# Opening loads of a fused attention and gated-MLP kernel: the first x tile in column halves from both queues, a new order of the first weight blocks, and a TensorE order to match

## The chip, the cores and the metric

The kernel runs on one core of one Trainium2 chip. The metric is the device time of one execution in microseconds. Before the change it is 206.2 us. The change touches only the first 6 us of the program and one later load, so everything here is about tenths of a microsecond; that is less than what one execution differs from the next, and part of the work is to tell the two apart.

## The reference, cut to what matters

```python
def _A_ref(x, wqkv, w_phi, wo):          # S=2048, D=512, H=32 heads of 16
    q, k, v = split(x @ wqkv)
    pq = einsum('bhsd,hdf->bhsf', q, w_phi)      # the kernel folds w_phi into wq and wk
    ...
def _B_ref(x, w_in, w_sp, b_sp, w_out):  # F = 1376 = 2*688
    z = gelu(x @ w_in)
    z1 = z[..., :688]
    z2 = layernorm(z[..., 688:])
    g = einsum('ts,bsf->btf', w_sp, z2) + b_sp
    return (z1 * g) @ w_out
g = sigmoid((x * gate_w).sum(-1, keepdims=True))
out = g * A + (1 - g) * B
```

The kernel starts with z2, the second half of `x @ w_in`. For that it needs x tiles transposed (`xT`) and four blocks of 128 rows of `w_in`, called blocks 0 to 3 of `w_z2` (172 KB each). The gate's weights ride along as one more column of `w_z2`: a small matmul turns `gate_w` into a column, and a copy puts it there.

## The kernel before

The opening loads, as issued from two queues (SyncE's, `nc.sync`, and ScalarE's, `nc.scalar`):

```python
nc.sync.dma_start(out=xs[:, 0, :], in_=x2[0:P, :])          # x tile 0, 128 KB
nc.scalar.dma_start(out=xs[:, 1, :], in_=x2[P:2 * P, :])    # x tile 1
load_z2w(nc.sync, 0)                                        # block 0 of w_z2
load_z2w(nc.scalar, 1)
load_z2w(nc.sync, 2)
nc.scalar.dma_start(out=gaterow[0:NDT, :], in_=gate_w...)
load_z2w(nc.sync, 3)
# ... a dummy gelu, to load ScalarE's table
x_dma_T(2, 2)            # transposing load of x tiles 2 and 3, SyncE
for h in range(2): ...   # w_z1, two loads, SyncE
for i in range(4, 8): x_dma_T(i)
# ... more transposing loads; brow; wqkT (two); w_phi (eight small loads); wv (two); w_sp
```

The opening on TensorE. `x_T` transposes pieces of an x tile into PSUM and a copy on VectorE (once ScalarE) brings them to `xT`; `one(t, b, j)` is the matmul of tile t, block b, column half j; `z_part` is half 1 of block 0 without the gate column, so that it needs no gate.

```python
warm_up(6)               # matmuls of constants, 512 columns
warm_up(1, P)            # and one of 128
x_T(0, 0, 1, ...); x_T(0, 1, NDT, ...)      # x tile 0
x_T(1, 0, 2, ...); x_T(1, 2, NDT, ..., on_act=True)
one(0, 0, 0); z_part(0, 0, HF, True)
gate_T()                 # gate column; the 345-column matmuls need its copy
one(0, 1, 0)
one(1, 0, 0); z_part(1, 0, HF, True)
one(1, 1, 0)
for tt in range(2): one(tt, 1, 1)           # the first with 345 columns
# ... blocks 2 and 3, then tiles 2, 3, ...
```

Much later, at 26 us, `fold` multiplies `wqkT` by `w_phi`; its first four matmuls together read all eight of the small w_phi loads.

The softmax here doesn't subtract the row's maximum and nothing guards it: scores larger than these inputs give would overflow.

## Time and profile before

| | before |
|---|---|
| time, median of 3 runs | 206.21 us (205.93 to 206.35) |
| TensorE busy | 200.8 of 204.5 us |
| first useful matmul | 4.54 us |
| tile 2's first matmul | 7.12 us |
| last w_phi landing; first fold matmul | 25.56; 25.93 us |

Two lines of the page: TensorE's busy time and the chain that ended last. TensorE (PE) is the chain, so every tenth that it starts later is paid at the end.

```profile
PE 200.8 (98%) x1557; PEld 119.9 (59%) x1557; DVE 130.4 (64%) x283; ACT 74.8 (37%) x122; POOL 45.6 (22%) x76
...
PE 98%; DVE 0%; issue 0%
```

Times inside an execution are counted from its first instruction. In text and tables the zero lies up to 0.01 us earlier than in the lines shown, so the last digit can differ by one.

The timeline of TensorE in the opening. Columns: start, duration of the group (us), engine, source line, operation, operands, count, and in brackets the idle time before it.

```profile
0.84 2.83 PE L222 MATMUL zp<-const-bfloat16-1.0 128*128 128x512 bf16 x7 [0.84 <-PEq L628]
3.46 0.63 PE L280 MATMUL pq<-ident,xs 128*128 128x128 bf16 x4
...
4.53 0.44 PE L191 MATMUL zp<-w_z,xT 128*128 128x344 bf16 x1
4.77 0.38 PE L230 MATMUL zp<-w_z,xT 128*128 128x344 bf16 x1
4.99 0.17 PE L290 MATMUL pq<-ident,gaterow 128*128 128x4 bf16 x1
5.02 0.45 PE L191 MATMUL zp<-w_z,xT 128*128 128x344 bf16 x2
```

A matmul's duration in the trace is longer than the step to the next one (0.31 us for a transpose here, where the next starts after 0.107), so waits are read from the distance between starts. The last transpose starts at 4.21 and the first useful matmul at 4.54: it waited for block 0, which the trace's semaphore events show landing at 4.50.

DMA traffic in the same stretch (columns: window, busy time of five engines, granted clock, DMA share, GB/s).

```profile
1.80:2.40 0.60, 0.60 (x3) 0.15 (x2) 0.48 (x3) 0.06 (x1) 0.56 (x4) 1.00 0.57 191
2.40:3.00 0.60, 0.60 (x3) 0.22 (x2) 0.00 (x0) 0.60 (x1) 0.24 (x1) 1.00 1.09 330
3.00:3.60 0.60, 0.60 (x5) 0.23 (x4) 0.00 (x0) 0.60 (x1) 0.00 (x0) 1.00 0.93 306
```

SyncE's queue, from the timeline: how long it takes to issue its loads. A plain load of 128 rows takes about 0.4 us to issue, a transposing load 1.2 us or more (the last of x 2.8); each is issued as soon as the one before is out, until the w_phi loads at 20 to 24 us.

```profile
0.81 0.39 SPq L119 DMA_DIRECT2D xs<-in_A_x_dram  x1
1.25 1.36 SPq L117 DMA_DIRECT2D w_z<-in_B_w_in_dram  x3
2.66 1.33 SPq L131 DMA_TRANSPOSE xT<-in_A_x_dram  x1
...
20.25 4.13 SPq L150 DMA_DIRECT2D wphi<-in_A_w_phi_dram  x8
```

### The profile page before, as it was taken

The page shows a single profiled execution, that of the slowest core. Times are in us where ns is not written, and L with a number is a line of the kernel's source. Part 1 is how long each engine was busy: PE and PEld are TensorE (multiplying, and loading weights), DVE is VectorE, ACT ScalarE, POOL GpSimd, SP SyncE. Part 2 cuts the span into 40 slices and gives each one's busy share as a digit, 9 for nine tenths or more (in the row PEclk, how much of TensorE's full clock was granted, in tenths as well). Part 3 has the DMA queues.
Part 4 walks back from the last instruction along what each step waited for, and adds up shares of the span by engine and source line. Part 5 has one row for each costly group of instructions (what it writes and reads, how often), then busy time and mean ns, then how long its engine had stood idle before and what let it go on. Part 6 is the DMA issues. An engine that isn't in the chain of part 4 may idle for free.

```text
span 204.5 us, 3996 instructions
## 1 busy us (share of the span) xinstructions
PE 200.8 (98%) x1557; PEld 119.9 (59%) x1557; DVE 130.4 (64%) x283; ACT 74.8 (37%) x122; POOL 45.6 (22%) x76
## 2 busy tenths in 40 slices
PE   8999999999999999999999999999999999999994
PEld 4666666655665555656565666555555555665642
DVE  4567484837977587979797789555566645633332
ACT  3566678796222333332424042222251136002303
POOL 3020202021523325334242442222204220200000
PEclk9999999999999999999999999999999999999999
DMA  6999699999999027940423219853567458552833
GB/s 194 252 205 171 80 151 290 146 278 247 256 249 213 3 38 182 287 94 16 75 48 45 51 38 120 154 109 64 105 161 80 90 113 183 63 96 51 156 64 104
DMA packets 89931, 27.22 MB, mean 133 GB/s; under 512 B 84184, under 2 KB 89912, under 8 KB 89912
## 3 DMA queue, kind: packets, MB, share of 16 engines
q1 hardware_dynamic: 87744, 24.99, 65.4%
q10 hardware_dynamic: 2168, 1.98, 3.5%
q8 instruction: 12, 0.20, 0.4%
q14 instruction: 7, 0.06, 0.1%
HBM read 4.15 MB, written 2.10 MB: 31 GB/s over the span
## 4 chain that ended last, share of the span: by engine, by line
PE 98%; DVE 0%; issue 0%
PE mm L454 37%; PE zp L191 18%; PE mm L355 14%; PE mm L515 9%; PE mm L509 7%; PE mm L395 7%; PE kvacc L411 2%; PE at L467 2%; PE zp L222 1%; PE mm L520 1%; PE zp L307 0%; PE pq L280 0%; PE at L478 0%; PE pq L307 0%; DVE ob L527 0%; PE zp L230 0%
## 5 line engine op out<-in xcount | busy, mean ns | idle before, releaser
L454 PE MATMUL mm<-z2all,wspT 128*128 128x344 bf16 x512 | 79.9, 309 | 0.0
L454 PEld LDWEIGHTS <-wspT 128*128 128x128 bf16 x512 | 49.0, 98 | 25.3
L191 PE MATMUL zp<-w_z,xT 128*128 128x344 bf16 (+1 forms) x254 | 38.1, 310 | 0.0
L359 ACT ACTIVATE eq<-mm 128x512 bf16<-128x512 f32 x32 | 17.4, 594 | 51.4 <-PE mm L355 25.7
L363 DVE TENSOR_REDUCE zs<-eq 128x64 f32<-128x1024 bf16 x16 | 19.5, 1220 | 20.0 <-ACT eq L359 20.0
L191 PEld LDWEIGHTS <-xT 128*128 128x128 bf16 x254 | 24.4, 98 | 11.8
L359 ACT ACTIVATE ek<-mm 128x512 bf16<-128x512 f32 x32 | 17.3, 600 | 27.1 <-PE mm L355 27.1
L459 DVE SCALAR_TENSOR_TENSOR ucat<-mm,bT,z1all 128x344 bf16<-128x344 f32 x32 | 17.4, 544 | 15.0 <-PE mm L454 15.0
L372 POOL TENSOR_TENSOR eq<-eq,ratio 128x512 bf16<-128x512 bf16 x16 | 16.9, 1055 | 44.6 <-DVE ratio L371 36.7
L531 ACT ACTIVATE ob<-mm,g_inv 128x512 bf16<-128x512 f32 (+1 forms) x15 | 10.1, 680 | 33.1 <-PE mm L520 28.5
L363 DVE TENSOR_REDUCE zs<-ek 128x64 f32<-128x1024 bf16 x16 | 19.3, 1209 | 2.8 <-ACT ek L359 2.8
L515 PE MATMUL mm<-wspT,uT 128*128 128x512 bf16 (+2 forms) x85 | 20.1, 367 | 0.0
L355 PEld LDWEIGHTS <-xT 128*128 128x128 bf16 x128 | 12.2, 98 | 12.0
L372 POOL TENSOR_TENSOR ek<-ek,ratio 128x512 bf16<-128x512 bf16 x16 | 16.9, 1056 | 2.2 <-DVE ratio L371 1.7
L509 PE MATMUL mm<-wspT,oT 128*128 128x512 bf16 (+2 forms) x68 | 16.6, 366 | 0.0
L355 PE MATMUL mm<-wq_p,xT 128*128 128x512 bf16 x64 | 16.4, 379 | 0.0
L395 PE MATMUL mm<-wv_sb,xT 128*128 128x512 bf16 x64 | 16.4, 379 | 0.0
L355 PE MATMUL mm<-wk_p,xT 128*128 128x512 bf16 x64 | 16.3, 379 | 0.0
L209 DVE BATCH_NORM_STATS2 bn<-z2all 128x6 f32<-128x344 bf16 x32 | 14.9, 501 | 0.0
L206 ACT ACTIVATE z2all<-zp 128x688 bf16<-128x688 f32 x16 | 11.8, 744 | 7.3 <-PE zp L191 7.2
L260 ACT ACTIVATE z1all<-zp 128x688 bf16<-128x688 f32 x16 | 11.9, 744 | 5.1 <-PE zp L191 4.6
L515 PEld LDWEIGHTS <-uT 128*128 128x128 bf16 x85 | 8.1, 98 | 9.4 <-issue 0.2
(77 smaller groups left out, 142.7 us busy)
## 6 DMA issues: line engine op xcount, KB each, us to landing
out_dram<-ob ACTq DMA_DIRECT2D x12, 128.0 KB, 2.4
wspT<-in_B_w_out_dram SPq DMA_DIRECT2D x2, 640.0 KB, 4.9
w_z<-in_B_w_in_dram SPq DMA_DIRECT2D x2, 344.0 KB, 4.7
w_z<-in_B_w_in_dram SPq DMA_DIRECT2D x3, 172.0 KB, 3.5
wv_sb<-in_A_wqkv_dram SPq DMA_DIRECT2D x2, 256.0 KB, 2.7
wspT<-in_A_wo_dram SPq DMA_DIRECT2D x2, 256.0 KB, 4.0
out_dram<-ob SPq DMA_DIRECT2D x3, 128.0 KB, 1.8
uT<-ucat SPq DMA_TRANSPOSE x16, 2.8
```

The source lines that it names most:

```text
L191: nc.tensor.matmul(zp[:, j, 0:n], lhsT=xT[:, dt, tt * P:(tt + 1) * P], rhs=wt[:, dt, j * HF:j * HF + n], start=(dt == 0), stop=(dt == NDT ...
L209: nc.vector.bn_stats(out=bn6[:, tt, j, :], in_=z2v[:, j, :])
L260: nc.scalar.activation(out=z1all[:, tt, :].rearrange("p (j n) -> p j n", j=2), in_=zp[:, :, 0:HF], func=AF.Gelu_apprx_tanh,)
L355: nc.tensor.matmul(ps[:, :], lhsT=xT[:, dt, tt * P:(tt + 1) * P], rhs=w[:, dt, :], start=(dt == 0), stop=(dt == NDT - 1))
L359: nc.scalar.activation(out=e[:, :, a, :], in_=ps[:, :].rearrange("p (h f) -> p h f", f=DH), func=AF.Exp, scale=1.0 - 2.0 * a)
L363: nc.vector.tensor_reduce(out=z[:].rearrange("p h a -> p (h a)"), in_=e[:].rearrange("p h a f -> p (h a) f"), axis=AX.X, op=ALU.add,)
L372: nc.gpsimd.tensor_tensor(out=e[:, :, 1, :], in0=e[:, :, 1, :], in1=ratio[:, :, None].to_broadcast([P, H, DH]), op=ALU.mult)
L395: nc.tensor.matmul(v_ps[:, :], lhsT=xT[:, dt, tt * P:(tt + 1) * P], rhs=wv_sb[:, dt, :], start=(dt == 0), stop=(dt == NDT - 1))
L454: nc.tensor.matmul(gp[:, 0:HF], lhsT=wspT[:, st, tt * P:(tt + 1) * P], rhs=z2all[:, st, j * HF:(j + 1) * HF], start=(st == 0), stop=(st == ...
L459: nc.vector.scalar_tensor_tensor(out=ucat[tt % NU][:, c0 + j * HF:c0 + (j + 1) * HF], in0=gp[:, 0:HF], scalar=bT[:, tt:tt + 1], in1=z1all[ ...
L509: nc.tensor.matmul(acc, lhsT=oTs[tt][:, g, :], rhs=wo_t[:, g, c0:c1], start=start and g == 0, stop=stop and g == NG - 1)
L515: nc.tensor.matmul(acc, lhsT=uTs[tt][:, i + ft, :], rhs=w_main[i][:, ft, c0:c1], start=start and ft == 0, stop=False)
```

## The change

Its intent: 128 KB instead of 256 KB of x ahead of the first transposes; tile 1 and block 0 travel beside each other, and TensorE does both tiles' block 0 before the gate. The two loads of wv become one.

```diff
-    nc.sync.dma_start(out=xs[:, 0, :], in_=x2[0:P, :])
-    nc.scalar.dma_start(out=xs[:, 1, :], in_=x2[P:2 * P, :])
-    load_z2w(nc.sync, 0)
-    load_z2w(nc.scalar, 1)
+    HD = D // 2
+    nc.sync.dma_start(out=xs[:, 0, 0:HD], in_=x2[0:P, 0:HD])
+    nc.scalar.dma_start(out=xs[:, 0, HD:D], in_=x2[0:P, HD:D])
+    nc.sync.dma_start(out=xs[:, 1, :], in_=x2[P:2 * P, :])
+    load_z2w(nc.scalar, 0)
+    load_z2w(nc.sync, 1)
+    nc.scalar.dma_start(out=gaterow[0:NDT, :], in_=gate_w...)
     load_z2w(nc.sync, 2)
-    nc.scalar.dma_start(out=gaterow[0:NDT, :], in_=gate_w...)
-    load_z2w(nc.sync, 3)
+    load_z2w(nc.scalar, 3)
 ...
-    for h in range(2):
-        nc.sync.dma_start(out=wv_sb[:, 2 * h:2 * h + 2, :], in_=A_wqkv[...])
+    nc.sync.dma_start(out=wv_sb[:, :, :], in_=A_wqkv[...])
 ...
-        warm_up(6)
-        warm_up(1, P)
-        x_T(0, 0, 1, ...); x_T(0, 1, NDT, ...)
+        warm_up(5)
+        warm_up(3, P)
+        x_T(0, 0, 2, ...); x_T(0, 2, NDT, ...)
+        warm_up(2, P)
         x_T(1, 0, 2, ...); x_T(1, 2, NDT, ..., on_act=True)
         one(0, 0, 0); z_part(0, 0, HF, True)
+        one(1, 0, 0); z_part(1, 0, HF, True)
         gate_T()
         one(0, 1, 0)
-        one(1, 0, 0); z_part(1, 0, HF, True)
         one(1, 1, 0)
```

More of the change, by code (lines that the diff above doesn't have):

```diff
@@ L117, in load_z2w @@
         eng.dma_start(out=w_z2[:, dt, 0:FH], in_=w_in_v[:, dt, FH:F])
-    nc.sync.dma_start(out=xs[:, 0, :], in_=x2[0:P, :])
-    nc.scalar.dma_start(out=xs[:, 1, :], in_=x2[P:2 * P, :])
-    load_z2w(nc.sync, 0)
-    load_z2w(nc.scalar, 1)
+    HD = D // 2
[4 more added lines that the diff above has]
+    load_z2w(nc.sync, 1)
+    nc.scalar.dma_start(out=gaterow[0:NDT, :], in_=gate_w.rearrange("(dt p) -> dt p", p=P))
     load_z2w(nc.sync, 2)
-    nc.scalar.dma_start(out=gaterow[0:NDT, :], in_=gate_w.rearrange("(dt p) -> dt p", p=P))
-    load_z2w(nc.sync, 3)
+    load_z2w(nc.scalar, 3)
     scrap = early.tile([P, 1], BF16, name="scrap")
@@ L150 @@
         nc.sync.dma_start(out=wphi[us, :, us], in_=heads[u])
-    for h in range(2):
-        nc.sync.dma_start(
-            out=wv_sb[:, 2 * h:2 * h + 2, :],
-            in_=A_wqkv[h * 2 * P:(h + 1) * 2 * P, 2 * D:3 * D].rearrange("(dt p) n -> p dt n", p=P),
-        )
+    nc.sync.dma_start(out=wv_sb[:, :, :], in_=A_wqkv[:, 2 * D:3 * D].rearrange("(dt p) n -> p dt n", p=P))
     for q in range(NCH):
@@ L232, in z_part @@
                 rhs=w_z2[:, 0, HF + c0:HF + c1], start=start, stop=False, skip_group_check=True)
-        warm_up(6)
-        warm_up(1, P)
-        x_T(0, 0, 1, pq_tile([P, 1, P], BF16)[:, :, :])
-        x_T(0, 1, NDT, pq_tile([P, 3, P], BF16)[:, :, :])
+        warm_up(5)
+        warm_up(3, P)
+        x_T(0, 0, 2, pq_tile([P, 2, P], BF16)[:, :, :])
+        x_T(0, 2, NDT, pq_tile([P, 2, P], BF16)[:, :, :])
+        warm_up(2, P)
         x_T(1, 0, 2, tp1[:, :, :])
@@ L241, in z2_first_two @@
         z_part(0, 0, HF, True)
+        one(1, 0, 0)
+        z_part(1, 0, HF, True)
         gate_T()
         one(0, 1, 0)
-        one(1, 0, 0)
-        z_part(1, 0, HF, True)
         one(1, 1, 0)
```

## The prediction

> **What bounds it now.** TensorE: busy 200.8 of 204.5 us, 98% of the chain that ended last (page of the profile). A change at the opening counts only by how much it moves the TensorE stream, 1:1 to the end.
>
> **The opening now (timeline, waits).** Warm-up matmuls run from 0.84 to 3.36 us. The x tiles' DMAs land at 3.41 (SyncE) and 3.58 (ScalarE); eight transposes issue 3.46 to 4.32; block 0 of w_z2 lands at 4.50 and the first useful matmul starts at 4.54. It waits for block 0. Clock: warm-ups of 512 columns come every 427 ns, transposes of 128 every 107 ns, both half rate; from about 4.73 a 344-column matmul comes every 145 ns. The Trainium skill, "TensorE: Matmul & The Clock Gate", Part 1, says the array starts at half rate and doubles after about 3.4 us of activity; the trace agrees (about 3.9 us). So time won before 4.73 is worth half. A second loss: the gate matmul waits for gaterow, about 0.08 us (weight load at 4.92).
>
> **What the change does there.** 128 KB of x instead of 256 KB stand before tile 0's landing; DMA moves about 310 GB/s from 1.84 us (windows), landing about 0.7 us after its bytes. Estimates: x tile 0 lands at 3.0 to 3.3, tile 1 at 3.8, block 0 at 4.1, block 1 at 4.9, block 2 at 5.6, block 3 at 5.3. Transposes start at about 3.25, the first useful matmul at about 4.3, 0.2 us earlier, half of it in slow clock; with the gate wait gone TensorE is 0.15 to 0.2 us ahead from 5 us on. The Trainium skill, "DMA: Bandwidth & Descriptors", Issuing engines are not separate DMA queues, says both queues share the same 16 engines; so I expect no bandwidth gain, only another order.
>
> **What it costs.** There are eight completion semaphores in rotation. Before, seven DMAs precede the transposing load of x tiles 2 and 3, which issues at 2.66 without waiting. Now eight precede it, and in the instruction order it waits for ScalarE's x half to land (3.1 to 3.3). SyncE's queue issues back to back until 24.4 us (its issue of one transposing load takes 1.2 us), so everything behind shifts by about 0.4 to 0.6 us. Most has slack: tiles 2 and 3 land at 6.77 by bandwidth, w_z1 needed later. But the last of eight w_phi loads lands at 25.56, and the first fold matmul starts at 25.93; TensorE's sequencer waited for that landing until 25.59. Slack is about 0.26 us, less with TensorE 0.2 us early. DMA is partly idle near 11.5 us (0.2 to 0.5 busy), so the shift isn't absorbed by a backlog. The fold then starts at 25.9 to 26.3: opening gain lost, up to 0.3 us of stall net. Merging the two wv loads comes behind w_phi: no effect (wv lands 27.2, needed after 44 us), but it keeps later semaphores in the same rotation.
>
> **Prediction.** 206.35 us, 80% range 205.85 to 206.75. Faster by over 2%: 0.005; within 2%: 0.985; slower by over 2%: 0.01.
>
> **What would show it.** Right: first useful matmul at 4.2 to 4.4; gate matmul without idle time; tiles 2 and 3's load issued at 3.1 to 3.3; last w_phi landing at 25.9 to 26.1; a TensorE gap of 0.2 to 0.5 us before the first fold; after it the stream 0 to 0.3 us later than before. Wrong: w_phi lands at 25.6 as before, no gap at the fold; then about 206.0.
>
> **What would make it wrong.** SyncE's delay absorbed where transposing loads are already blocked (the loads at 11.87 and 15.37 took 2.4 to 2.8 us to issue); ScalarE's half landing before 2.9; tile 1 or block 2 landing late, stalling TensorE and delaying the clock; run-to-run spread of 0.4 us hiding everything.

## The result

| | before | after |
|---|---|---|
| time, median of 6 runs | 206.23 us (205.88 to 206.50) | 206.53 us (206.22 to 206.93) |
| ratio after to before | | 1.0018 (95% 1.0003 to 1.0033) |
| x tile 0 landed | 3.41 us | 2.83 and 3.05 (halves) |
| x tile 1 landed | 3.58 | 4.36 |
| block 0 landed | 4.50 | 4.55 |
| first useful matmul | 4.54 | 4.64 |
| tile 2's first matmul | 7.12 | 7.34 |
| last w_phi landing; first fold matmul | 25.56; 25.93 | 25.96; 26.19 |

A ratio is the mean time of one kernel's fast runs over that of the other's in the same rounds, so it is not quite the ratio of the medians. 1.0018 is +0.37 us. A second measurement (the control r9 below) gave 1.0019. The rows below the ratio come from one profiled execution each.

The page lines of after; the chain now has a DMA in it, the load of an x tile.

```profile
PE 200.6 (98%) x1560; PEld 119.9 (59%) x1560; DVE 130.4 (64%) x283; ACT 74.6 (36%) x122; POOL 45.8 (22%) x76
...
PE 96%; DMA 2%; SPq 0%; DVE 0%; issue 0%
```

The timeline of TensorE after. Tile 0's transposes come 0.21 us earlier, as intended. Then TensorE has two short warm-ups and stands idle for tile 1.

```profile
3.25 0.63 PE L279 MATMUL pq<-ident,xs 128*128 128x128 bf16 x4
3.67 0.38 PE L220 MATMUL zp<-const-bfloat16-1.0 128*128 128x128 bf16 x2
4.39 0.29 PE L279 MATMUL tp<-ident,xs 128*128 128x128 bf16 x2 [0.34 <-DMA xs<-in_A_x_dram]
4.52 0.28 PE L279 MATMUL pq<-ident,xs 128*128 128x128 bf16 x2
4.63 0.31 PE L189 MATMUL zp<-w_z,xT 128*128 128x344 bf16 x1
4.77 0.31 PE L228 MATMUL zp<-w_z,xT 128*128 128x344 bf16 x1
5.06 0.32 PE L189 MATMUL zp<-w_z,xT 128*128 128x344 bf16 x1
```

Two steps of 0.29 us stand where a 344-column matmul takes 0.145: from 4.78 to 5.07, and from 5.55 to 5.84. VectorE's timeline shows both reasons: the copy of tile 1's transposes ends at 5.01, and the copy of the gate column at 5.78, just ahead of the 345-column matmul.

```profile
4.72 0.29 DVE L285 COPY xT<-tp 128x256 bf16<-128x256 bf16 x1 [0.51 <-PE tp L279]
5.60 0.17 DVE L290 CAST w_z<-pq 128x4 bf16<-128x4 f32 x1 [0.59 <-PE pq L289]
```

And the likely reason why tile 1 lands later than the 3.8 us of the prediction: the same windows of DMA traffic. From 2.4 to 3.0 us only 115 GB/s flow, where before had 330. The missing 215 GB/s over 0.6 us are 129 KB, about the size of x tile 1.

```profile
1.80:2.40 0.60, 0.60 (x3) 0.15 (x1) 0.48 (x3) 0.00 (x0) 0.56 (x4) 1.00 0.78 213
2.40:3.00 0.60, 0.60 (x3) 0.22 (x2) 0.00 (x0) 0.28 (x1) 0.24 (x1) 1.00 0.72 115
3.00:3.60 0.60, 0.60 (x8) 0.60 (x7) 0.00 (x0) 0.60 (x1) 0.00 (x0) 1.00 1.00 334
```

SyncE's queue after. The transposing load issues at 3.06 instead of 2.66: there are eight completion semaphores, taken in turn (the trace shows their numbers), this is now the ninth load of the hardware queues, and it waits until ScalarE's half of x has landed. The shift is still 0.3 us at the last transposing load of x (12.17 instead of 11.86), 0.12 at the first of wqkT (15.49 for 15.37), 1.10 at the second (18.95 for 17.85) and 0.37 at the last w_phi load (24.33 for 23.96). So it does not run down the queue unchanged: the transposing loads from 12 to 20 us take 1.7 to 3.4 us each to issue in these two traces, not the same in both, and one trace against another does not tell how much of the shift arrives. Over all profiles the last w_phi load issued at 22.83 to 24.02 us in the six kernels without the wait (before, r1, r3, r7, r8, r12) and at 23.03 to 25.08 in the seven with it apart from r4.

```profile
0.80 0.40 SPq L120 DMA_DIRECT2D xs<-in_A_x_dram  x1
1.25 0.42 SPq L122 DMA_DIRECT2D xs<-in_A_x_dram  x1
1.72 0.90 SPq L117 DMA_DIRECT2D w_z<-in_B_w_in_dram  x2
3.06 1.32 SPq L133 DMA_TRANSPOSE xT<-in_A_x_dram  x1
```

At the fold nothing is lost: in both traces the first fold matmul starts 0.242 us after the last matmul before it, as it does in r1, where w_phi had landed 2.6 us earlier. TensorE arrives 0.26 us late and finds w_phi landed. Its weight loads at the fold, before and after; neither waits for a DMA:

```profile
25.93 0.56 PEld L307 LDWEIGHTS <-wqkT 32*128 32x128 bf16 x64 [0.28 <-issue]
26.18 0.56 PEld L306 LDWEIGHTS <-wqkT 32*128 32x128 bf16 x64 [0.28 <-issue]
```

**The sum in these two traces.** The first useful matmul is 0.10 us later; the two waits for copies cost 0.145 each; the clock gives back some 0.19 us, because in this execution it switched to full rate at 3.90 us (in the one of before at 4.92, so that TensorE's useful work began at half rate, and (4.92 - 4.54)/2 = 0.19 was lost there). 0.10 + 0.29 - 0.19 = 0.20; measured at tile 2: 0.22. Another 0.04 comes at 10 us, where the second load of w_z1 lands only at 10.26 (9.55 before). Of these 0.26 us, 0.13 are back by 37 us. That is no gain of the change: near the end of the second fold of before one matmul stands 0.13 us after its predecessor (36.44 to 36.57), a hole that after doesn't have, and r1, r2, r6, r7, r9 and r12 neither. What made it, the trace doesn't say. So the two profiled executions end only 0.14 us apart (spans of 204.50 and 204.64), while the mean loss is 0.37.

**When the clock switches.** The page shows the granted clock as 1.00 from the start, but the warm-ups of 512 columns come every 427 ns, and later work shows 2.4 columns a nanosecond: the first microseconds run at half rate. The trace's clock record begins where the switch comes, and the record of full clock is 201.386 us long in before, after and eight others, 59 times 3.413, and 197.973 in r1 and r5, 58 times; the two lengths differ by 3.413 us (r8 and r10 have no record). The Trainium skill, "TensorE: Matmul & The Clock Gate", Part 1, says that the gate watches a free-running window of 3413 ns; the records agree. So the switch falls at a different time in each execution, and one trace against another can mislead by some tenths of a microsecond.

The prediction read the switch of before at 4.73 us, because the first 344-column matmul was followed after 0.24 us instead of 0.287. But the first step after a wait is that short at half rate too (r5: 5.50 to 5.74, with half rate until 8.99). By the record it came at 4.92, 4.1 us after the first warm-up.

Counting windows of 3.413 us back from the switch gives a rule of thumb, inferred from three traces only. In after, the window that ended with the switch (0.48 to 3.90) held 0.36 us of idleness, ahead of the first warm-up. In r1 the window before the switch (0.14 to 3.55) held 0.70 us, and in r5 (2.17 to 5.58) the wait of 0.97 us for block 0; at the end of neither did the clock switch. So here 0.7 us of idleness in a window put the switch off by one window, and 0.36 did not.

### The profile page after: what moved, and what is told of

The parts are those of the page before. It is cut to its first block, busy times and chain, and to the rows that moved or that the text cites. A ratio compares the mean times of both kernels' runs of the same rounds, so it can differ in the third digit from the quotient of the medians.

```text
span 204.6 us, 4002 instructions
## 1 busy us (share of the span) xinstructions
PE 200.6 (98%) x1560; PEld 119.9 (59%) x1560; DVE 130.4 (64%) x283; ACT 74.6 (36%) x122; POOL 45.8 (22%) x76
## 4 chain that ended last, share of the span: by engine, by line
PE 96%; DMA 2%; SPq 0%; DVE 0%; issue 0%
PE mm L453 37%; PE zp L189 18%; PE mm L354 14%; PE mm L514 8%; PE mm L508 7%; PE mm L394 7%; PE kvacc L410 2%; PE at L466 2%; DMA xs<-in_A_x_dram 2%; PE mm L519 1%; PE zp L306 0%; PE at L477 0%; SPq L120 0%; PE pq L306 0%; DVE ob L526 0%; PE zp L228 0%
## 5 line engine op out<-in xcount | busy, mean ns | idle before, releaser
L189 PEld LDWEIGHTS <-xT 128*128 128x128 bf16 x254 | 24.4, 98 | 12.3 <-DVE xT L285 0.3
```

The source lines that it names most:

```text
L189: nc.tensor.matmul(zp[:, j, 0:n], lhsT=xT[:, dt, tt * P:(tt + 1) * P], rhs=wt[:, dt, j * HF:j * HF + n], start=(dt == 0), stop=(dt == NDT ...
```

## The experiments

All ran five rounds beside the kernel before on the same chip; the times are medians of 5 or 6 executions. The first four shared one chip, the next four another, the last four a third. Fast runs only; one run of before (209.03) counts as slow, since it is over 1.5% above the fastest of its kernel, and is left out. The three long executions of r5 (208.63 to 208.91) and the two of r7 (208.73, 209.24) stay under that line and are in the ratios, so those two ratios say little about the usual execution.

| run | time | before there | ratio (95%) |
|---|---|---|---|
| r1, changed TensorE order only | 206.61 | 206.12 | 1.0027 (1.0010 to 1.0043) |
| r2, changed loads only | 206.78 | 206.12 | 1.0031 (1.0019 to 1.0043) |
| r3, changed, x tile 0 whole | 206.94 | 206.12 | 1.0043 (1.0029 to 1.0057) |
| r4, before with an extra small load | 207.02 | 206.12 | 1.0044 (1.0030 to 1.0058) |
| r5, both x tiles in halves | 207.73 | 206.27 | 1.0068 (1.0030 to 1.0106) |
| r6, changed, gate earlier | 206.62 | 206.27 | 1.0016 (0.9995 to 1.0036) |
| r7, changed, no semaphore wait | 206.95 | 206.27 | 1.0063 (1.0020 to 1.0107) |
| r8, before with block 0 in halves | 207.03 | 206.27 | 1.0031 (1.0014 to 1.0048) |
| r9, changed, again | 206.77 | 206.60 | 1.0019 (0.9996 to 1.0042) |
| r10, changed, wait filled | 207.01 | 206.60 | 1.0026 (1.0008 to 1.0045) |
| r11, r5 with the wait filled | 207.06 | 206.60 | 1.0028 (1.0009 to 1.0047) |
| r12, before, gate later | 206.24 | 206.60 | 0.9995 (0.9974 to 1.0017) |

### r1: the TensorE order alone

Before's loads, with the TensorE lines of the diff above.

> The kernel before with only the changed TensorE order (gate matmul after both tiles' first four block-0 matmuls, x tile 0 copied in two pairs, five long and five short warm-ups); loads as before. Theory P (the order itself costs): the 345-column matmul of block 1 again waits for the copy of the gate column, a hole of 0.14 us, and the first useful matmul stays at about 4.55 us; tile 2's first matmul about 0.15 us later than before, time +0.1 to +0.2 us. Rival L (all of the loss comes from the loads): no hole, time within 0.05 us of before. DMA stays at 300 GB/s or more from 2.4 to 3.0 us in both.

Measured: 206.61 us, six executions from 206.05 to 207.18. DMA traffic 308 GB/s from 2.4 to 3.0 us, tile 1 at 3.57. The profiled execution was the slowest (207.18): its clock switched only at 6.97 us, so the opening matmuls came every 287 ns and hid every copy. The mean loss is larger than expected and the expected hole could not be seen. What follows: the order is not free, but this run doesn't show by what; r6 shows one part. It may also show how large the clock's part is: the same program took 206.05 and 207.18, though only the slowest execution was profiled.

### r2: the loads alone

The changed kernel with before's TensorE lines.

> The changed kernel with the TensorE order of before; loads as changed. Theory H (the half-width loads of x tile 0 run out before the next loads' packets flow): the hole in DMA traffic from 2.4 to 3.0 us stays (about 115 GB/s against 330), tile 1 lands at 4.3 to 4.4, block 0 at 4.5 to 4.6, the first useful matmul comes at about 4.65. The gate comes early, so the wait for its copy (0.14 us) is gone: time +0.05 to +0.2 over before, about 0.14 less than the changed kernel. If the loads were the whole loss (rival L), it is as slow as the changed kernel, +0.3.

Measured: 206.78 us, +0.3%, more than expected and no better than the changed kernel. Traffic from 2.4 to 3.0 us 194 GB/s, tile 1 at 4.08 and block 0 at 4.26, the first useful matmul at 4.49, the gate's copy in time. The landings are 0.2 to 0.3 us earlier than expected. But block 2 landed at 6.50 (5.45 in the profile of after) and TensorE stood for it:

```profile
6.53 0.45 PE L189 MATMUL zp<-w_z,xT 128*128 128x344 bf16 x2 [0.58 <-DMA w_z<-in_B_w_in_dram]
```

So the loads by themselves lose what the whole change loses. The order by itself does so too (r1), and the intervals overlap: the parts do not add up, and the times do not divide the loss between the two. Which block is late differs between executions (in r9, the same loads, block 2 landed at 6.32).

### r3: x tile 0 whole, from SyncE

```diff
-    nc.sync.dma_start(out=xs[:, 0, 0:HD], in_=x2[0:P, 0:HD])
-    nc.scalar.dma_start(out=xs[:, 0, HD:D], in_=x2[0:P, HD:D])
+    nc.sync.dma_start(out=xs[:, 0, :], in_=x2[0:P, :])
```

> The changed kernel with x tile 0 loaded whole from SyncE; the rest of the new load order and the TensorE order kept (two loads of wv, so that the rotation of semaphores is that of before). Theory H: no hole, at least 280 GB/s from 2.4 to 3.0 us; x tile 0 lands at about 3.4, tile 1 at about 4.1, block 0 before 4.1; first useful matmul at about 4.4 and time 0.1 to 0.25 us less than the changed kernel. Rival B (tile 1 is slow because it shares the engines with block 0): tile 1 still lands at 4.3 or later and the first useful matmul at 4.6, time as the changed kernel.

Measured: 206.94 us. The dip at 2.4 to 3.0 us is gone, tile 1 lands at 4.06 and block 0 at 3.73, as theory H says. The traffic of r3 (the same columns as above), with a dip in the very first window instead:

```profile
1.80:2.40 0.60, 0.60 (x3) 0.15 (x2) 0.48 (x3) 0.16 (x1) 0.57 (x4) 1.00 0.90 103
2.40:3.00 0.60, 0.60 (x3) 0.22 (x2) 0.00 (x0) 0.60 (x1) 0.24 (x1) 1.00 0.87 313
```

The time isn't better: the clock switched at 5.63 us, the first useful matmul came at 4.63, and block 1 landed at 6.13 (4.89 after), for which TensorE stood 0.44 us. The expectation for the time failed. What follows: rival B (tile 1 is slow because it travels beside block 0) is unlikely, since here it does so and lands 0.3 us earlier, though block 0 had a start of one load; and moving a wait to another block gains nothing.

### r4: the fold's slack, measured by a delay

The kernel before; one 1 KB load, its data unused, on ScalarE's queue, so that the transposing load of tiles 2 and 3 is the ninth.

```diff
+    nc.scalar.dma_start(out=spare[0:NDT, :], in_=gate_w...)
```

> The kernel before with one extra 1 KB load on ScalarE's queue (its data are not used), as the eighth ahead of the transposing load of x tiles 2 and 3, which then waits for x tile 1 to land; wv in one load, so that later semaphores keep their rotation. The TensorE opening is untouched. Theory F (the fold has about 0.26 us of slack behind the last w_phi landing): the transposing load issues at about 3.6 instead of 2.66, the last w_phi lands at about 26.4 to 26.5, TensorE has a new gap of 0.5 to 0.7 us before the first fold and the time is +0.5 to +0.7 us. Rival (the delay is absorbed where transposing loads are blocked at issue): last w_phi lands at 25.6 to 25.8, no gap, time within 0.1 us.

Measured: 207.02 us, +0.9. The load issued at 3.49, 0.83 later than before; the last w_phi landed at 27.17 (expected 26.4 to 26.5). TensorE's weight loads in the fold of r4:

```profile
26.16 0.14 PEld L305 LDWEIGHTS <-wqkT 32*128 32x128 bf16 x3 [0.28 <-issue]
27.27 0.56 PEld L305 LDWEIGHTS <-wqkT 32*128 32x128 bf16 x61 [0.97 <-DMA wphi<-in_A_w_phi_dram]
```

Three go at once; the fourth needs the last two heads and waits 0.97 us for w_phi. So theory F's mechanism is real: a late queue can stop TensorE at the fold. Its size was off: the wait was 1.0 instead of 0.5 to 0.7 us. It isn't the shift of 0.83 carried through: that had become 0.66 at the load of brow and 1.95 at the first of wqkT, as brow took 1.80 us to issue (0.51 before), for a reason that is not known. Nor is all of the 0.9 us the fold's: in this profile block 0 landed at 4.80, and tile 2 began 0.24 us later than before. The slack that I had read as 0.26 us isn't a constant either: in r1, with the same queue program as before, the last w_phi landed at 24.44, 1.1 us earlier than in the profile of before.

### r5: halves beside halves

```diff
+    for i in range(2):
+        nc.sync.dma_start(out=xs[:, i, 0:HD], in_=x2[i * P:(i + 1) * P, 0:HD])
+        nc.scalar.dma_start(out=xs[:, i, HD:D], in_=x2[i * P:(i + 1) * P, HD:D])
     load_z2w(nc.sync, 0); load_z2w(nc.scalar, 1); load_z2w(nc.sync, 2)
+    nc.gpsimd.dma_start(out=gaterow[0:NDT, :], in_=gate_w...)
     load_z2w(nc.scalar, 3)
```

> Both x tiles in column halves from both queues (x beside x, then block 0 beside block 1 as before), gaterow moved to GpSimd's queue, TensorE order of before. The halves are as short as in the changed kernel, but an x load never starts beside a w_in block. Theory H (short loads run dry): the dip in DMA traffic at 2.4 to 3.0 us (under 200 GB/s) stays. Theory W (the dip comes where an x tile starts on SyncE beside a w_in block on ScalarE, as it did in the changed kernel and at 2.1 to 2.4 us with x tile 0 whole): at least 280 GB/s from 2.4 to 3.0 us, tile 1 lands before 3.7, block 0 at 4.4 to 4.6; opening as before, time within 0.3 us of before.

Measured: both theories failed in part. The dip is not at 2.4 to 3.0 us but one window later, where the four x loads have ended and the first w_in blocks must take over:

```profile
2.40:3.00 0.60, 0.60 (x3) 0.21 (x2) 0.00 (x0) 0.28 (x1) 0.58 (x6) 1.00 1.13 280
3.00:3.60 0.60, 0.60 (x5) 0.32 (x4) 0.00 (x0) 0.60 (x1) 0.38 (x3) 1.00 0.64 91
```

Halves following halves run without a break, so short loads do not make the dip by themselves (against H as written); and no x load starts beside a w_in block here (against W). Block 0 landed at 5.46. The times fall into two levels: 206.64, 206.73, 206.83, and 208.63, 208.65, 208.91. The profiled one was of the upper level; its timeline of TensorE:

```profile
5.50 0.45 PE L189 MATMUL zp<-w_z,xT 128*128 128x344 bf16 x1 [0.97 <-DMA w_z<-in_B_w_in_dram]
5.74 0.49 PE L228 MATMUL zp<-w_z,xT 128*128 128x344 bf16 x1
...
6.91 1.65 PE L189 MATMUL zp<-w_z,xT 128*128 128x344 bf16 x5
```

After 1 us of idleness the matmuls keep the half rate (287 ns apart, from 6.91 on) until the clock's switch at 8.99 us. That suggested theory C, tested by r9 to r11.

### r6: the gate ahead of tile 1

```diff
         one(0, 0, 0); z_part(0, 0, HF, True)
-        one(1, 0, 0); z_part(1, 0, HF, True)
         gate_T()
+        one(1, 0, 0); z_part(1, 0, HF, True)
         one(0, 1, 0)
```

> The changed kernel with the gate matmul moved ahead of tile 1's two block-0 matmuls, nothing else. Theory P (the late gate puts the copy of the gate column before the 345-column matmul of block 1): the 0.29 us step there becomes 0.15 (or stays 0.29 only where the clock is still at half rate), and the wait for tile 1's copy may shrink too; 0.1 to 0.2 us less than the changed kernel. Rival (another wait ends just as late): no step of 0.29 there, but tile 2 starts no earlier.

Measured: tile 1 at 4.32 and block 0 at 4.52, as in after, and the clock at full rate before the first useful matmul in both, so the two traces can be compared. The step of 0.29 us at the 345-column matmul is gone, and tile 2 starts at 7.23 instead of 7.34. The wait for tile 1's copy is now 0.12 us, behind the gate:

```profile
4.82 0.31 PE L228 MATMUL zp<-w_z,xT 128*128 128x344 bf16 x1
4.97 0.17 PE L289 MATMUL pq<-ident,gaterow 128*128 128x4 bf16 x1
5.12 0.32 PE L189 MATMUL zp<-w_z,xT 128*128 128x344 bf16 x1
```

So the late gate costs about 0.1 us in the trace. In the times (1.0016 against 1.0018 and 1.0019) that is too small to show.

### r7: no wait for the semaphore

The changed kernel with `gaterow` loaded from GpSimd's queue.

> The changed kernel with gaterow on GpSimd's queue: seven hardware-queue loads precede the transposing load of x tiles 2 and 3, so it no longer waits. Theory F as predicted (the shift of SyncE's queue costs time at the fold): the load issues at 2.66 again, the last w_phi lands 0.4 us earlier, and the time falls by 0.1 to 0.4 us against the changed kernel. Theory N (in the changed kernel TensorE is itself late, so the fold never waited): w_phi lands earlier, no change in time beyond 0.1 us; the dip of DMA traffic at 2.4 to 3.0 us and tile 1's landing at 4.1 to 4.4 us stay.

Measured: the transposing load issues at 2.66 and the last w_phi lands at 25.23. The fold still starts 0.243 us after the matmul before it, and the time is not lower: theory N, not the prediction's. The dip is there (160 GB/s), tile 1 lands at 4.13. The run is not clean: from GpSimd's queue gaterow landed at 5.18 us (4.24 in after), and the gate matmul waited for it until 5.23. Two of six executions took 208.73 and 209.24, the others 206.31 to 207.03 (a mean 0.36 us above before's, as for the changed kernel); the two weren't profiled, so what they waited for is open. r5 suggests the clock.

### r8: block 0 in halves, a try for a better version

```diff
+    for eng, c in ((nc.sync, 0), (nc.scalar, HF)):
+        eng.dma_start(out=w_z2[:, 0, c:c + HF], in_=w_in_v[:, 0, FH + c:FH + c + HF])
```

(x tiles whole, as before; gaterow from GpSimd; block 1 on SyncE, 2 on ScalarE, 3 on SyncE; the gate after tile 1's first matmul.)

> A try for a version better than both: the kernel before (x tiles whole, one on each queue) with block 0, the load that ends the wait for the first useful matmul, in column halves from both queues, gaterow on GpSimd's queue, and the gate after tile 1's first matmul. Expected: block 0's first half lands at about 4.0 instead of 4.5, the first useful matmul at 4.35 instead of 4.54, no wait for gaterow; time 0.1 to 0.25 us less than before. Rival (halves of a load start no sooner, because the skew between the DMA engines decides the landing): the half lands at 4.4 or later, time within 0.1 us of before.

Measured: 207.03 us, slower than before. The first half landed at 4.30, the first useful matmul came at 4.44, 0.1 us earlier than before, and then block 1 landed at 5.82 and TensorE stood for it. The expectation failed: what block 0 gains, block 1 loses.

### r9, r10, r11: does the clock make the loss?

r9 is the changed kernel as it is. r10 has `warm_up(7, P)` for `warm_up(2, P)`; r11 is r5 with `warm_up(10, P)` before `one(0, 0, 0)`.

> The changed kernel itself, as a control on the chip of the next three. Expected 0.1 to 0.6 us slower than before, the dip of DMA traffic at 2.4 to 3.0 us and tile 1's landing at 4.1 to 4.4 us again. Theory C (the wait for tile 1 leaves TensorE idle for about 0.5 us, and the clock's switch[...] is sometimes put off by a whole window): some executions at 207 or above.

> The changed kernel with seven short warm-up matmuls instead of two before tile 1's transposes, so that TensorE is busy while it waits. Theory C: the spread shrinks (no execution above 206.9) and the mean falls by 0.1 us or more against the changed kernel on this chip. Rival (the loss is the late landing of tile 1 and block 0 and the two waits for copies, whatever the clock does): mean within 0.1 us of the changed kernel.

> The kernel with both x tiles in halves, which took 206.6 to 206.8 in three executions and 208.6 to 208.9 in three others, with ten short warm-ups in the 1.3 us in which TensorE waited for block 0. Theory C: the executions at 208.6 and above are those in which the idle stretch spoiled a window of the clock, so they vanish: all within 206.4 to 207.4. Rival (the two levels come from the DMA): still two levels, about 2 us apart.

Measured. r9: ratio 1.0019, as in the first measurement; dip 86 GB/s, tile 1 at 4.20, and steps of 0.29 us at the same two copies. Some executions were above 207, but so was one of before on this chip. r10: 207.01 and 1.0026; filling the wait does not help (the mean is 0.2 us above r9's, where the rival had said within 0.1), so theory C is not the changed kernel's loss. Tile 1 landed at 4.58 in its profile, the dip was 41 GB/s, and for 0.2 us in it not one packet started on either queue.

r11: five executions between 207.05 and 207.11. The upper level of r5 is gone and with it nearly all spread. So there theory C fits: the wait for block 0, 1.0 us of idleness, had sometimes put the switch of the clock off (to 8.99 us in the profile of r5; 5.01 in that of r11). The DMA does not explain it: block 0 and the dip are as late and as deep in r11. Two reserves: r5 was not repeated on r11's chip, and only one execution of r5 was profiled. One line of r11's timeline: the first useful matmul, with the short wait that is left.

```profile
5.57 0.31 PE L189 MATMUL zp<-w_z,xT 128*128 128x344 bf16 x1 [0.18 <-DMA w_z<-in_B_w_in_dram]
```

r11 is still slower than before, for its block 0 lands at 5.53.

### r12: the gate later in the kernel before, a second try

Before's loads; two short warm-ups ahead of `one(0, 0, 0)`, and `gate_T()` after `one(0, 1, 0)`.

> A try for a version better than both: the kernel before, loads untouched, with two short warm-ups in the wait for block 0 and the gate matmul after tile 0's first block-1 matmul, where gaterow has landed. Expected: no wait for gaterow (0.08 us), time 0.05 to 0.15 us less than before, at the edge of what five rounds can show. Rival: block 1's landing takes the place of the wait, no change.

Measured: 0.9995 (0.9974 to 1.0017), no difference that can be seen; 0.08 us would be too small for this interval in any case. The wait of 0.08 us for gaterow, which it was to remove, was misread, as the trace of before shows: in the profile of before the 344 columns ahead of the gate matmul began at half rate and ended at full rate (the switch at 4.92 us), and that alone makes the step of 0.22 us. The weight load waited for gaterow, the matmul did not.

No version beats the kernel before.

### What is left open

The dip of DMA traffic. With the new loads it came in all six profiles (after and r2, r6, r7, r9, r10: 41 to 194 GB/s from 2.4 to 3.0 us), with the other arrangements in none of eight (280 to 364). r5 and r11 have it one window later (91 and 83). The kernels with two whole x tiles first (before, r1, r4, r8, r12) have none at that hand-over. So it comes where short x loads end and longer ones follow, and half-width loads that follow half-width loads don't show it. Being short is not enough: in r8 half-width loads of block 0 are followed by whole blocks, at 285 and 306 GB/s from 3.0 to 4.2 us. In the dip of after some of the first packets of the next loads take very long, up to 0.65 us where the median of such packets is 0.046 (r10: up to 1.04); r9 has none over 0.34, but a stretch of 0.25 us in which no packet started. What holds the next loads back, no run shows; r3 and r12 also have a slow first window (103 and 60 GB/s from 1.8 to 2.4), so a part of it may belong to the start of any program.

## Why the prediction was right or wrong

The total was right, the sum under it only in part. Predicted 206.35, measured 206.53: slower by a little, inside the range, for a reason that was not the one given. That the number fits is partly luck: the range of 0.9 us also holds before's 206.2, and a predicted gain at the opening with a stall at the fold was in fact a loss at the opening without a stall.

- **Bound by TensorE, 1:1 to the end.** Right: 96% of the chain after the change, and the 0.26 us stays to the end but for a hole in before's second fold.
- **Tile 0's half loads: "x tile 0 lands at 3.0 to 3.3".** Right, even a little early: 2.83 and 3.05; transposes at 3.25 as predicted.
- **"tile 1 at 3.8, block 0 at 4.1".** Wrong, and this is the step that failed. The estimate took 310 GB/s from 1.84 us on. The runs showed 115 GB/s from 2.4 to 3.0 us, and 4.36 and 4.55. The first useful matmul came at 4.64 instead of "about 4.3", and "TensorE is 0.15 to 0.2 us ahead from 5 us on" became 0.22 behind. The prediction had named this itself among what would make it wrong ("tile 1 or block 2 landing late, stalling TensorE").
- **"with the gate wait gone".** Wrong twice. There was no such wait for the matmul (the trace of before, under r12), and the gate's later place put its copy on the path: 0.145 us in the trace, 0.11 at tile 2 by r6. I had looked at what the gate waits for, not at who waits for the gate. Tile 1's copy, another 0.145, I had missed as well.
- **SyncE's shift: "waits for ScalarE's x half", "shifts by about 0.4 to 0.6 us", "last w_phi landing at 25.9 to 26.1".** The wait is right: 3.06 us, and in all eight profiles where eight loads stand ahead the transposing load issues 0.02 us after the landing of ScalarE's first load. The rest is right in the numbers, 0.40 at the head and 25.96 at the end, but the agreement is partly luck: in between the shift shrank to 0.12 and grew to 1.10, and with the same loads the last w_phi landed at 24.65 us in r2 and 26.09 in r9.
- **"a TensorE gap of 0.2 to 0.5 us before the first fold".** Not seen: TensorE was itself 0.26 us late and met w_phi landed. The mechanism is real (r4: a wait of 0.97 us), but in the changed kernel it cost nothing, and taking the shift away gained nothing (r7).
- **Both queues share the same 16 engines, so no bandwidth is gained.** The Trainium skill, "DMA: Bandwidth & Descriptors", Issuing engines are not separate DMA queues. The runs fit this: at full flow about 300 to 390 GB/s in every arrangement, and each version that brought one landing forward (r3, r8) had another later.
- **wv in one load: no effect.** Nothing in the trace speaks against it; no run had it alone.

## What to carry to other kernels

Splitting the first load brought its bytes sooner here (x tile 0 at 3.05 instead of 3.41 us), but the loads behind it were not yet flowing when it ended: look at the traffic in windows of half a microsecond, not only at the bytes ahead in the queue. When a small producer (here the gate column) is moved later to spare its own wait, check who reads its result and when. And where a warm-up covers a wait, a clock that switches at a different time in each execution (3.90 to 6.97 us here) makes single traces differ by more than the change: compare waits in the trace, and times over many executions.

## What the Trainium skill lacked or had wrong

- "TensorE: Matmul & The Clock Gate", Part 1, puts the switch at about 4 us of activity with a spread of 500 ns either way. With the first warm-up at 0.85 us in all, it came here between 3.90 us (after) and 6.97 us (r1), r5 apart; the spread of 3.07 us is nearly the window's whole length. The page's window of 3413 ns itself agrees with the records (201.386 us = 59 windows).
- The same page gives idle gaps of some 3 us as the danger for a warm clock. It asks for continuous work to reach full rate, but doesn't say how short a gap during warm-up can put the switch off: with 1.0 us idle, r5 switched at 8.99 us, and half of its executions took 2 us more; with the gap filled (r11) all were within 0.06 us.
- "DMA: Bandwidth & Descriptors", Issuing engines are not separate DMA queues, calls the sequencer's issue time usually small relative to the DMA. Here a transposing load of 128 rows takes 1.2 to 1.3 us to issue, of 4 to 5 us to its landing, SyncE's queue is issuing almost without pause from 0.8 to 24.4 us, and in r4 its last w_phi load came so late that TensorE stood for 0.97 us.
- On no page did I find the hand-over between short first loads and longer ones: traffic of 41 to 194 GB/s for 0.6 us where whole tiles gave 283 or more.
